# Scanning the decays once on compact rows and multiplying them into B and C before their transposes

## The chip, the cores and the metric

The kernel runs on one core of a Trainium2 chip. The metric is the device time of one launch in microseconds (us), and lower is better. Executions of one kernel spread by about 1% or more, and the medians of the same kernel differ by up to 1% (the kernel before: 140.49 to 141.62 us). So every experiment below was timed in rounds beside the kernel before on the same chip, and its ratio to that kernel is given with the median. A run that is more than 1.5% above the fastest of its kernel is counted as slow and is left out of the ratios; only fast runs are compared with fast runs.

Names: PE is TensorE, DVE is VectorE, ACT is ScalarE, POOL is GpSimd. SP and ACT also issue the loads. PSUM is where the matmuls of this kernel leave their results, HBM is the memory of the chip from which the loads come.

## The reference, cut to what matters

```python
# x (4, 8, 768, 32), a (4, 8, 768), B and C (4, 8, 768, 16), all fp32
la  = np.log(np.clip(a, 1e-6, 1.0))                  # decay of every token of every head
for c in chunks:                                     # state-space layer, chunk by chunk
    cum = np.cumsum(la[chunk]);  L = exp(cum_i - cum_j) * causal
    y   = ((C B^T) * L) x + (C state) * exp(cum)
    state = exp(sum la) * state + sum_j B_j x_j exp(cum_end - cum_j)
h   = y_as_3072_tokens_by_256 @ w_in                 # MLP: 256 -> 2048
out = gelu_tanh(h) @ w_out                           # 2048 -> 256
```

The kernel takes chunks of 128 tokens, so there are 4 batches of 6 chunks. In every chunk a decay factor is split in two: `r` (the product of decays from a token to the end of its chunk) scales B, and its inverse `pn` (up to a factor of the chunk) scales C. Both come out of a running product, a scan.

## The kernel before

The program builds a list of pieces of work with an engine, an estimated duration and a priority. A small scheduler (`run_order`) puts them into one order before anything runs; each engine then executes its own list in that order (in b_wo_first below PE stood 3.30 us at the entry that came next in its list; in b_fill_hole, with other work put ahead of that entry, PE was busy for 10.07 us of that window of 12.9 us instead of 7.79). Dummy matmuls ("fillers", 128x512, into a bank that nobody reads) are put into gaps of PE that the scheduler foresees in the first 22 us.

For every batch the parts that the change touches are these. The decays are loaded 16 times over, once for every state row, so that they lie in the layout [128 = head x state, 768 tokens]. DVE scans them in this layout, twice.

```python
def load_a(b, t0, t1):                       # 16-fold replicated: [0, N] is a stride of zero
    nc.sync.dma_start(out=d["a"][:, t0:t1],
        in_=bass.AP(tensor=a.tensor, offset=..., ap=[[S, H], [0, N], [1, t1 - t0]]))

def f_R(b, c0, c1):                          # DVE: clip, scan from the right, two small ones
    nc.vector.tensor_scalar(out=ac[:, s0:e1], in0=d["a"][:, s0:e1], ...)
    nc.vector.tensor_tensor_scan(out=d["r"][:, s0:s1][:, ::-1], data0=ac[...][:, ::-1], ...)
    ...
def f_P(b, c0, c1):                          # DVE: scan from the left
    nc.vector.tensor_tensor_scan(out=d["pn"][:, s0:s1], data0=a_cl[b % 2][:, s0:s1], ...)

def f_castbc(b, i, eng, r0, r1): ...         # B or C to bf16, token-major
def f_T(b, i): ...                           # PE: six 128x128 transposes into PSUM
def f_E(b, i, p0, p1):                       # DVE: out of PSUM, multiplied by r or pn
    nc.vector.tensor_tensor(out=tv(d[nm]), in0=d[("t", i)]..., in1=tv(d[("r", "pn")[i]]),
                            op=ALU.mult)
# then: F  (DVE)  C split by head parity -> ce        N (PE) B back to token-major
#       G  (PE)   Gram matmuls -> gb                  M (DVE) causal mask, PSUM -> m
#       Y  (PE)   output of a chunk -> yb             S, SP (DVE) running state
#       s1 (PE)   first MLP layer, line L391          s2 (PE) second MLP layer, line L409
```

Some short names are used below and in the expectations: "first MLP matmul" or s1 is the first `hp<-xm,w_in_sb` matmul, T the transposes of B and C, M0 the mask of chunk 0, and G, Y as above.

## Time and profile before

| | before |
|---|---|
| median (3 runs) | 141.21 us (141.12 to 141.3) |
| span of the profiled run | 140.0 us |
| busy PE / DVE / ACT / POOL | 121.4 / 78.3 / 80.5 / 17.0 us |
| read from HBM | 12.06 MB |
| first MLP matmul starts | 19.60 us |
| last matmul ends | 136.41 us |

The first view is the page's row of slices: 40 equal slices of the span (3.5 us each), each digit the busy share in tenths; PEclk is the granted clock of TensorE in tenths.

```profile
PE   6583799961599969899989999999999999999990
...
DVE  2538999709985499999799676788200000000011
...
PEclk9999999996558999999999999999999999999999
```

Counted from 0, PE is dense from slice 20 on. The losses lie before: the start, and a hole in slices 8 to 10; the clock falls in slices 9 to 12. DVE is nearly full from slice 14 to slice 21.

The second view is the chain of waits, the work that ended last followed back to its releasers, as shares of the span by engine.

```profile
PE 60%; DMA 17%; DVE 16%; ACT 2%; SPq 1%; issue 1%; DVEq 0%; ACTq 0%
```

Three of the longer pieces of the same chain in order of time (start, length, what):

```profile
2.74 8.09 DMA a_t<-in_a_dram
...
21.70 9.45 DMA a_t<-in_a_dram
...
41.38 6.25 DMA a_t<-in_a_dram
```

Three loads of the replicated decays make up the 17% of DMA. The third view is the timeline of DVE around the second of them (start, length, engine, line, what; in brackets the idle time before it and what ended it).

```profile
31.17 0.56 DVE L228 TENSOR_SCALAR ac_120<-a_t 128x768 f32<-128x768 f32 x1 [4.12 <-DMA a_t<-in_a_dram]
31.77 1.76 DVE L236 TENSOR_TENSOR_SCAN r_t<-ac_120,ends 128x768 f32<-128x768 f32 x1
...
33.72 0.55 DVE L214 CAST bc_551<-bc_t 128x768 bf16<-128x768 f32 x1
34.19 1.75 DVE L253 TENSOR_TENSOR_SCAN pn_t<-ac_120,headz 128x768 f32<-128x768 f32 x1
...
37.91 0.88 DVE L214 CAST w_out_sb<-wf 128x1024 bf16<-128x1024 f32 x1
```

The timeline of PE, with the first MLP matmul and the end of the wait in that stretch:

```profile
19.60 1.08 PE L391 MATMUL hp<-xm,w_in_sb 128*128 128x128 bf16 x16
...
34.33 0.82 PE L273 MATMUL hp<-ident,bc_551 128*128 128x128 bf16 x6 [3.83 <-DVE bc_551 L214]
```

The same stretch in the table of windows: start and end, length, then the busy time with the number of instructions for PE, PEld (weight loads), DVE, ACT and POOL, then the granted clock, the share of DMA and GB/s.

```profile
30.50:43.40 12.90, 7.28 (x64) 5.97 (x65) 10.54 (x17) 3.51 (x8) 4.21 (x6) 0.60 0.56 97
```

DVE stood 4.12 us for the decays of batch 1, then scanned. PE stood 3.83 us for the first cast of that batch, and in 12.9 us it was busy for 7.28 us at a mean clock of 0.60. The last w_out cast came only at 37.91.

### The profile page before, as it was taken

What the parts mean: (1) busy time and instruction counts of PE and PEld (TensorE: products, weight loads), DVE (VectorE), ACT (ScalarE), POOL (GpSimd) and SP (SyncE); (2) the same over time, 40 slices, a digit from 0 to 9 for tenths busy, and PEclk for the clock granted to TensorE, in tenths of its full rate; (3) what the DMA queues carried; (4) which work ended last, traced back from release to release, by engine and by line L of the source; (5) the groups of instructions that cost most, each with busy time, mean ns of one, the idle gap of its engine ahead of it and who ended that gap; (6) DMA issues with size and microseconds to landing.
All of it is one profiled execution on the core that took longest, in us unless ns stands there. A gap on an engine that the chain in (4) does not pass through costs nothing.

```text
span 140.0 us, 3321 instructions
## 1 busy us (share of the span) xinstructions
PE 121.4 (87%) x1380; PEld 94.4 (67%) x1380; DVE 78.3 (56%) x143; ACT 80.5 (58%) x161; POOL 17.0 (12%) x36
## 2 busy tenths in 40 slices
PE   6583799961599969899989999999999999999990
PEld 2141368751477857687867776777888888888870
DVE  2538999709985499999799676788200000000011
ACT  4124858670154844258835877687877777777210
POOL 7200023101810023112131110000000000000000
PEclk9999999996558999999999999999999999999999
DMA  2999999998705997898611010101011111111121
GB/s 64 243 211 326 308 275 265 223 162 146 110 21 148 218 158 141 178 254 155 96 37 42 0 37 5 37 0 42 0 37 42 37 37 37 42 37 37 62 90 37
DMA packets 40630, 15.41 MB, mean 110 GB/s; under 512 B 33832, under 2 KB 39080, under 8 KB 40616
## 3 DMA queue, kind: packets, MB, share of 16 engines
q1 hardware_dynamic: 39576, 14.82, 47.4%
q10 hardware_dynamic: 1040, 0.39, 1.1%
q8 instruction: 10, 0.16, 0.6%
q14 instruction: 4, 0.03, 0.1%
HBM read 12.06 MB, written 3.15 MB: 109 GB/s over the span
## 4 chain that ended last, share of the span: by engine, by line
PE 60%; DMA 17%; DVE 16%; ACT 2%; SPq 1%; issue 1%; DVEq 0%; ACTq 0%
PE o_ps L409 25%; PE hp L391 24%; DMA a_t<-in_a_dram 17%; DVE r_t L236 4%; DVE m L324 3%; PE yb L341 3%; PE gb L316 3%; PE hp L409 2%; DVE pn_t L253 2%; PE yb L335 1%; ACT gT L399 1%; PE hp L273 1%; DVE ch L285 1%; DVE bh L285 1%; DVE ac_118 L228 1%; DVE bc_551 L214 1%
## 5 line engine op out<-in xcount | busy, mean ns | idle before, releaser
L399 ACT ACTIVATE gT<-hp 128x512 bf16<-128x512 f32 x96 | 55.3, 598 | 25.2 <-PE hp L391 24.3
L391 PE MATMUL hp<-xm,w_in_sb 128*128 128x256 bf16 (+1 forms) x480 | 56.4, 255 | 0.4 <-ACT gT L399 0.2
L409 PE MATMUL o_ps<-w_out_sb,gT 128*128 128x256 bf16 x352 | 50.6, 277 | 1.1 <-ACT o_sb L416 1.1
L391 PEld LDWEIGHTS <-w_in_sb 128*128 128x128 bf16 x480 | 39.1, 99 | 6.7 <-issue 1.1
L409 PEld LDWEIGHTS <-gT 128*128 128x128 bf16 x384 | 36.6, 99 | 6.8 <-issue 1.7
L324 DVE TENSOR_TENSOR m<-gb,tri 128x1024 bf16<-128x1024 f32 x24 | 29.2, 1218 | 2.4 <-PE gb L316 2.4
L418 DVE COPY o_sb<-o_ps 128x256 f32<-128x256 f32 x2 | 0.8, 424 | 36.8 <-PE o_ps L409 36.8
L359 ACT ACTIVATE xm<-yb 128x256 bf16<-128x256 f32 x24 | 9.2, 382 | 6.3 <-PE yb L352 4.6
L590 PE MATMUL o_ps<-wz 128*128 128x512 bf16 x36 | 11.0, 436 | 1.3 <-DVE warm L124 1.3
L416 ACT ACTIVATE o_sb<-o_ps 128x256 f32<-128x256 f32 x20 | 7.6, 380 | 5.7 <-PE o_ps L409 5.4
L372 DVE SCALAR_TENSOR_TENSOR sp_new<-s_new,pend,bmask 128x256 bf16<-128x256 f32 x20 | 9.5, 477 | 0.2
L316 PE MATMUL gb<-ce,bh 32*128 32x256 bf16 x96 | 6.9, 278 | 2.1 <-DVE m L324 1.2
L210 ACT ACTIVATE w_in_sb<-wf 128x1024 bf16<-128x1024 f32 x4 | 4.2, 1057 | 4.8 <-DMA wf<-in_moe_w_in_dram 4.8
L316 PEld LDWEIGHTS <-bh 32*128 32x128 bf16 x96 | 2.7, 91 | 6.0 <-issue 5.2
L590 PEld LDWEIGHTS <-wz 128*128 128x128 bf16 x36 | 3.4, 107 | 4.9 <-issue 1.6
L273 PE MATMUL hp<-ident,bc_551 128*128 128x128 bf16 x12 | 1.6, 307 | 5.5 <-DVE bc_551 L214 3.8
L366 DVE SCALAR_TENSOR_TENSOR s_new<-s_new,pend,yb 128x64 f32<-128x64 f32 x16 | 4.4, 274 | 3.4 <-ACT xm L359 2.9
L309 ACT ACTIVATE bn<-yb 128x384 bf16<-128x384 bf16 (+2 forms) x9 | 4.1, 454 | 3.4 <-DVE w_out_sb L214 2.2
L335 PE MATMUL yb<-ch,sp_new 128*128 128x128 bf16 x40 | 5.7, 225 | 0.0
L273 PEld LDWEIGHTS <-bc_551 128*128 128x128 bf16 x12 | 1.2, 135 | 5.8 <-DVE bc_551 L214 4.9
L285 DVE TENSOR_TENSOR ch<-hp,pn_t 128x768 bf16<-128x768 bf16 (+3 forms) x6 | 4.1, 682 | 0.8 <-PE hp L273 0.8
L285 DVE TENSOR_TENSOR bh<-hp,r_t 128x768 bf16<-128x768 bf16 (+3 forms) x6 | 4.1, 680 | 0.6 <-PE hp L273 0.6
(147 smaller groups left out, 89.5 us busy)
## 6 DMA issues: line engine op xcount, KB each, us to landing
x_t<-in_x_dram SPq DMA_DIRECT2D x24, 128.0 KB, 4.3
out_dram<-o_sb SPq DMA_DIRECT2D x24, 128.0 KB, 1.7
wf<-in_moe_w_in_dram SPq DMA_DIRECT2D x4, 512.0 KB, 8.4
wf<-in_moe_w_out_dram SPq DMA_DIRECT2D x4, 512.0 KB, 8.0
bc_t<-in_C_dram SPq DMA_DIRECT2D x4, 384.0 KB, 6.4
a_t<-in_a_dram SPq DMA_DIRECT2D x3, 384.0 KB
bc_t<-in_B_dram SPq DMA_DIRECT2D x3, 384.0 KB, 6.8
bc_t<-in_B_dram ACTq DMA_DIRECT2D x1, 384.0 KB
```

Source lines behind the costliest of these rows:

```text
L236: nc.vector.tensor_tensor_scan(out=d["r"][:, s0:s1][:, ::-1], data0=ac[:, s0 + 1:s1 + 1][:, ::-1], data1=ef[:, ::-1], initial=1.0, op0=ALU ...
L285: nc.vector.tensor_tensor(out=tv(d[nm]), in0=d[("t", i)].rearrange("q (r p) -> q p r", r=R6)[:, p0:p1], in1=tv(d[("r", "pn")[i]]), op=ALU. ...
L316: nc.tensor.matmul(out=gb[:, g, 0:256], lhsT=d["bh"][32 * g:32 * g + 32, c * Q:(c + 1) * Q], rhs=d["ce"][32 * g:32 * g + 32, c].rearrange( ...
L324: nc.vector.tensor_tensor(out=m, in0=gram, in1=tri_b, op=ALU.mult)
L335: nc.tensor.matmul(out=y_ps[:, w], lhsT=sp[:, w * 128:(w + 1) * 128], rhs=d["ch"][:, c * Q:(c + 1) * Q], start=(w == 0), stop=False, skip_ ...
L359: nc.scalar.activation(xm[:, :, gc * Q:(gc + 1) * Q], y_ps, AF.Copy)
L372: nc.vector.scalar_tensor_tensor(out=sp_new.rearrange("p (g d) -> p g d", g=4), in0=state[("s", gc)].rearrange("p (o d) -> p o d", o=1).to ...
L391: nc.tensor.matmul(out=hp[:, j * nt:(j + 1) * nt], lhsT=w_in_sb[:, kc, fi * 128:(fi + 1) * 128], rhs=xm[:, kc, c0 * Q:c0 * Q + nt], start= ...
L399: nc.scalar.activation(gts[g][:, i * per:(i + 1) * per, 0:nt], hps.pop((g, i)).rearrange("p (j t) -> p j t", j=per), AF.Gelu_apprx_tanh)
L409: nc.tensor.matmul(out=ops[gc], lhsT=gts[g][:, fi, tt * Q:(tt + 1) * Q], rhs=w_out_sb[:, fi, :], start=(fi == 0), stop=(fi == NF - 1), ski ...
L416: nc.scalar.activation(o_sb, ops.pop(gc), AF.Copy)
L590: nc.tensor.matmul(out=zb, lhsT=wz[:, 0:128], rhs=wz, start=True, stop=True)
```

## The change

Intent: load the decays once, compactly (64 rows of 384, 0.1 MB instead of 1.57 MB), clip and scan them once for all batches, and only from the right. Small fp32 matmuls against an identity ("RT") bring the scan's result to token-major, one number for each token and head; `1/r` is a reciprocal. These factors are multiplied into B and C in the place of the casts, ahead of the transposes, so that what comes out of PSUM is only copied. Four more fp32 matmuls ("pp") spread the chunks' end factors `pend`. The order of loads changes, weight casts move to POOL, and the scheduler gets a rule for letting DVE and POOL stand still for a more urgent piece that is nearly ready. Much is cut here:

```diff
+    a_t = const.tile([64, HS], FP32, name="a_t")
+    nc.scalar.dma_start(out=a_t[0:32], in_=a_half[0])
+    load_bc(0, 1, nc.sync)
+    nc.scalar.dma_start(out=a_t[32:64], in_=a_half[1])
+    load_bc(0, 0, nc.sync)
 ...
-    def f_P(b, c0, c1):  ... (second scan, gone)
-    def f_castbc(b, i, eng, r0, r1):  ... (cast, gone)
+    def f_R():
+        nc.vector.tensor_tensor_scan(out=r_t[:, ::-1], data0=ac[:, 1:HS + 1][:, ::-1], ...)
+    def f_RT():                               # 12 fp32 matmuls
+        for r in range(R6):
+            for i in range(2):
+                nc.tensor.matmul(out=U[0]["rp"][64 * i:64 * i + 64, r],
+                                 lhsT=r6[32 * i:32 * i + 32, r], rhs=idf[...], ...)
+    def f_pp():                               # 4 fp32 matmuls
+        for b in range(batch):
+            nc.tensor.matmul(out=U[0]["pp"][:, b * CPB:(b + 1) * CPB], lhsT=selp[...], ...)
+    def f_mul(b, i, eng, r0, r1):             # in place of the cast
+        (nc.vector if eng == "DVE" else nc.gpsimd).tensor_tensor(
+            out=d["bc16"][:, i, r0:r1], in0=d["bc"]..., in1=w..., op=ALU.mult)
 ...
     def f_E(b, i, p0, p1, eng):
-        nc.vector.tensor_tensor(out=tv(d[nm]), in0=..., in1=tv(d[("r", "pn")[i]]), op=ALU.mult)
+        copy(eng, d[nm]..., d[("t", i)]...)
 ...
+    weng = [("POOL", "ACT", "POOL", "DVE"), ("POOL", "POOL", "POOL", "DVE")]   # w_in, w_out
 ...
+            if b == 0:      # first batch: both multiplies split between DVE and POOL
+                ms = [add("DVE", 0.6, f_mul, b, i, "DVE", 0, 4, deps=dp, prio=-62 - i),
+                      add("POOL", 0.7, f_mul, b, i, "POOL", 4, R6, deps=dp, prio=-62 - i)]
 ...
-    for t, fn in run_order(nodes, pools, idle=idle):
+    for t, fn in run_order(nodes, pools, idle=idle, wait=("DVE", "POOL")):
```

## The prediction

> **What bounds it now.** Time is a PE (TensorE) stream that starts late and is interrupted once. In the timeline the first matmul of the two-layer MLP starts at 19.6 us and the last ends near 136.4; span 140.0, median 141.2. From 80 us on the table of windows shows PE 100% busy. Two losses lie earlier.
> 1. Start: until 19.6 us PE does fillers and small matmuls. The chain there is DMA `a_t` (arriving 10.85), then DVE clip, scans, E, F, M in pieces, M for chunk 0 only at 12.19, M for chunk 1 at 17.86.
> 2. The hole 30.5-43.4 us. DVE waits 4.1 us (view of waits) for batch 1's `a_t`, issued at 21.7, landed 31.17, a 16-fold replicated 384 KB load; then in order clip 0.56, scan 1.76, cast, scan 1.75, cast 0.69, E 0.94, and only then the last `w_out` cast at 37.91, for which every second-layer group waits. PE does about 4.5 us of full-clock work in 12.9 us. [...] A hole of 2 us at 49-51.6 is the same scan again.
>
> **What changes.** Removed from DVE: about 7.4 us each of the r and p scans, 2.2 clips, 4.8 of B/C casts, three of four w_out casts (2.2). From DMA: 1.57 MB of replicated `a` becomes 0.1 MB. Added: one clip and 64x384 scan (0.35 + 0.96, as the 128x384 ones), 12 fp32 matmuls (estimate 1 us), reciprocals 0.5 + 1.3, multiplies in place of casts (estimate 0.9 each against 0.65, from E's 0.94). PSUM copies replace E at about equal cost. Net DVE 78 to about 62 us. POOL gains five weight casts, estimate 1.6 us each undisturbed (four times 0.40), ACT loses three.
>
> **New start (estimate).** a lands 3.3, scan ends 4.8, matmuls 5.9, C lands near 5.7, multiply 7.0, transposes, F, G0 near 9, M0 ends 10.6, Y0 11, first MLP matmul near 12, 7.5 us sooner. Then arrivals pace it: at the 2.36 us per x-plus-wo pair seen now, the last w_in lands near 14.5, the last w_out near 22-23, B/C of batch 1 near 27, all before PE runs dry.
>
> **Sum.** PE work left after 43.4 us is 93 us less about 3 us of waits, plus 18 us done before: 108 us. If after has done 12-14 us of it by 22-23 us and then runs dense with 1-2 us of gaps, PE ends near 118-119; tail 3.6, span to median 1.2: about 123.5 us, 12.5% less. About 8 us comes from closing the holes, the rest from the early start; the DVE saving itself is mostly off the critical path.
>
> **What the profile would show.** First MLP matmul at 11-14 us; no a_t wait on DVE after 4 us; PE clock 0.9+ throughout 20-60; a chain almost all PE after about 23 us; scan time about 1 us; DVE busy 60-65.
>
> **What would make it wrong.** POOL is slow: an x cast (0.40 alone) took 1.2-1.7 beside DVE casts and scans. [...] If weight casts take 3-4 us, x3 and w_out come late, and a new hole opens at 18-27 us (+3 to 6 us). In-order DVE waits (for the fourth w_in cast, before M2) could delay chunks 2 and 3.
>
> Range 119.5-129; faster 0.97, same 0.02, slower 0.01.

93 us less 3 us plus 18 us make 108 us of work on PE, which was to end near 118 to 119, and 3.6 and 1.2 us more make about 123.5 us. What the trace of the kernel before shows of the clock in the hole is 0.57, 0.50 and 0.65 from 32 to 36, 36 to 40 and 40 to 44 us. The trace of the kernel after has 1.57 us for the 12 fp32 matmuls (predicted 1), 0.46 and 1.04 us for the reciprocals (0.5 and 1.3), 0.95 to 1.08 us for a multiply of a whole batch on DVE (0.9), and 0.95 us for a copy of 128x768 out of PSUM on DVE, the time of E before.

## The result, and the profile after

| | before | after |
|---|---|---|
| median of this comparison (4 runs each) | 141.17 us | 129.51 us |
| all runs | 140.65 to 141.3 | 128.77, 129.07, 129.96, and a slow one of 130.76 |
| ratio of the fast runs | | 0.9163, 95% interval 0.9102 to 0.9225 |
| span of the profiled run | 140.0 us | 127.1 us |
| busy PE / DVE / ACT / POOL | 121.4 / 78.3 / 80.5 / 17.0 | 118.9 / 66.9 / 77.2 / 21.4 |
| read from HBM | 12.06 MB | 10.58 MB |
| first MLP matmul starts | 19.60 | 17.96 |
| last matmul ends | 136.41 | 123.82 |
| from one to the other | 116.8 | 105.9 |

A ratio here and below is the mean time of one kernel's fast runs over the mean of the other's fast runs of the same rounds, so it is not quite the ratio of the medians quoted beside it.

The change is 8.4% faster. The predicted direction was right. The predicted 123.5 us was not: the measured 129.5 us is just outside the range of 119.5 to 129.

First the slices of the page, 3.2 us each:

```profile
PE   6579899899999999999999999999999999999990
...
DVE  2354899877978799899956658665000000000001
...
PEclk9985559999999999999999999999999999999999
```

The chain of waits by engine:

```profile
PE 86%; DMA 3%; DVE 3%; ACT 3%; issue 1%; ACTq 0%; DVEq 0%
```

The window that answers to the hole shown before:

```profile
30.50:43.40 12.90, 12.90 (x198) 10.76 (x195) 10.99 (x16) 8.19 (x18) 2.96 (x7) 1.00 0.91 174
```

The hole is gone: PE is busy 12.90 of 12.90 us at full clock, and the chain is nearly all PE. That is the last row of the table: the stretch from the first MLP matmul to the last matmul fell from 116.8 to 105.9 us. What did not come is the early start. The clock's row shows where one cause lies: slices 3 to 5, from about 10 to 19 us, stand at half. The timeline of DVE in the first 20 us:

```profile
5.59 0.35 DVE L245 TENSOR_SCALAR ac<-a_t 64x384 f32<-64x384 f32 x1 [2.05 <-DMA a_t<-in_a_dram]
5.97 0.95 DVE L249 TENSOR_TENSOR_SCAN r_t<-ac,ends 64x384 f32<-64x384 f32 x1
...
9.17 0.69 DVE L294 TENSOR_TENSOR bc_181<-bc_t,pt 128x512 bf16<-128x512 f32 x1
9.78 1.11 DVE L294 TENSOR_TENSOR bc_181<-bc_t,rt 128x512 bf16<-128x512 f32 x1
...
18.18 1.45 DVE L235 CAST w_in_sb<-wf 128x1024 bf16<-128x1024 f32 x1
```

And the timeline of PE:

```profile
7.07 1.57 PE L260 MATMUL hp<-idf,r_t 32*64 32x32 f32 x24 [2.21 <-DVE r_t L249]
8.57 1.89 PE L650 MATMUL o_ps<-wz 128*128 128x512 bf16 x4
10.39 1.87 PE L281 MATMUL hp<-pe_112,selp 64*128 64x6 f32 x8
12.19 1.46 PE L309 MATMUL hp<-ident,bc_181 128*128 128x128 bf16 x12
...
16.92 1.03 PE L650 MATMUL o_ps<-wz 128*128 128x512 bf16 x2
...
17.96 1.36 PE L428 MATMUL hp<-xm,w_in_sb 128*128 128x128 bf16 x16
```

Four things are to be seen. The clip, and with it everything, waited until 5.59 for the compact decays. The four fillers took 1.89 us, which is half pace: the kernel before ran four of them in 1.04 us at 13.68. The pp matmuls stand in front of the transposes for 1.87 us. And the last two fillers, 1.03 us at half pace, stand directly in front of the first MLP matmul (two transposes between).

That it is half, although 1.89 is less than twice 1.04, is an estimate from longer runs of fillers in the same traces. The kernel after took 3.59 us for its first eight, so four more cost 1.70 us; the kernel before took 1.90 us for eight at 16.84, so four more cost 0.86 us. By that, one more filler takes about 0.43 us at half pace and 0.22 us at full pace. In the expectations below, cold stands for half pace.

The trace records two rows for each of the fp32 matmuls (24 for the 12 of RT, 8 for the 4 of pp). Their price was 1.57 us for RT and 1.87 us for pp, against an estimate of 1 us for RT in the prediction and none for pp. The 1.87 us is the price at half pace: in the run best below, where PE was at full pace from 6.39 us on, pp took 1.02 us, while RT, which ran before that, took 1.54 us.

Some instructions of DVE took longer beside POOL. Two lines of the timeline of POOL:

```profile
9.22 1.12 POOL L294 TENSOR_TENSOR bc_181<-bc_t,pt 128x256 bf16<-128x256 f32 x1 [4.88 <-DVE pt L267]
...
18.04 1.04 POOL L233 CAST w_out_sb<-wf 128x1024 bf16<-128x1024 f32 x1 [0.37 <-DMA wf<-in_moe_w_out_dram]
```

The w_in cast took 1.45 us at 18.18, after POOL had begun to cast w_out at 18.04; the same cast took 0.68 us in a_first below, where no POOL cast overlapped it, and 0.68 us in control, where it began 0.36 us before POOL's. The C multiply on DVE began 0.05 us before POOL's part of it and took 0.69 us; the B multiply of the same shape began while POOL's part of C still ran, took 1.11 us, and ended 0.55 us after that part (10.34). The B multiply reads two tiles (`bc_t` and `rt`), the cast only one; why either took longer here, no run shows.

### The profile page after: what moved, and what is told of

Read it like the earlier page. It is cut to its first block, busy times and chain, and to the rows that moved or that the text cites. A ratio compares the mean times of both kernels' runs of the same rounds, so it can differ in the third digit from the quotient of the medians.

```text
span 127.1 us, 3322 instructions
## 1 busy us (share of the span) xinstructions
PE 118.9 (94%) x1393; PEld 95.2 (75%) x1394; DVE 66.9 (53%) x109; ACT 77.2 (61%) x159; POOL 21.4 (17%) x45
## 3 DMA queue, kind: packets, MB, share of 16 engines
HBM read 10.58 MB, written 3.15 MB: 108 GB/s over the span
## 4 chain that ended last, share of the span: by engine, by line
PE 86%; DMA 3%; DVE 3%; ACT 3%; issue 1%; ACTq 0%; DVEq 0%
PE hp L428 33%; PE o_ps L446 31%; PE gb L352 4%; PE yb L377 4%; PE o_ps L650 3%; DMA a_t<-in_a_dram 3%; PE hp L446 3%; PE hp L309 3%; ACT gT L436 2%; PE yb L371 2%; PE hp L281 1%; PE hp L260 1%; PE yb L338 1%; DVE m L360 1%; DVE sp_new L409 1%; DVE r_t L249 1%
## 5 line engine op out<-in xcount | busy, mean ns | idle before, releaser
L428 PE MATMUL hp<-xm,w_in_sb 128*128 128x256 bf16 (+1 forms) x480 | 54.6, 253 | 0.3 <-ACT gT L436 0.2
L446 PE MATMUL o_ps<-w_out_sb,gT 128*128 128x256 bf16 x352 | 48.6, 273 | 0.1
L409 DVE SCALAR_TENSOR_TENSOR sp_new<-s_new,pend,bmask 128x256 bf16<-128x256 f32 x20 | 10.3, 514 | 0.6
L650 PE MATMUL o_ps<-wz 128*128 128x512 bf16 x17 | 8.2, 626 | 1.3 <-DVE warm L153 1.3
L650 PEld LDWEIGHTS <-wz 128*128 128x128 bf16 x18 | 2.0, 129 | 4.0 <-issue 2.7
L446 PE MATMUL hp<-w_out_sb,gT 128*128 128x256 bf16 x32 | 3.8, 272 | 0.2 <-ACT gT L436 0.2
L371 PEld LDWEIGHTS <-sp_new 128*128 128x128 bf16 x40 | 3.6, 98 | 0.5
L235 DVE COPY ch<-hp 128x768 bf16<-128x768 bf16 x4 | 3.8, 948 | 0.0
L260 PEld LDWEIGHTS hp<-idf,r_t 32*64 32x64 f32 x24 | 1.5, 201 | 3.1 <-issue 3.1
## 6 DMA issues: line engine op xcount, KB each, us to landing
x_t<-in_x_dram SPq DMA_DIRECT2D x24, 128.0 KB, 3.8
out_dram<-o_sb SPq DMA_DIRECT2D x24, 128.0 KB, 1.7
```

The source lines that it names most:

```text
L371: nc.tensor.matmul(out=y_ps[:, w], lhsT=sp[:, w * 128:(w + 1) * 128], rhs=d["ch"][:, c * Q:(c + 1) * Q], start=(w == 0), stop=False, skip_ ...
L409: nc.vector.scalar_tensor_tensor(out=sp_new.rearrange("p (g d) -> p g d", g=4), in0=state[("s", gc)].rearrange("p (o d) -> p o d", o=1).to ...
L428: nc.tensor.matmul(out=hp[:, j * nt:(j + 1) * nt], lhsT=w_in_sb[:, kc, fi * 128:(fi + 1) * 128], rhs=xm[:, kc, c0 * Q:c0 * Q + nt], start= ...
L446: nc.tensor.matmul(out=ops[gc], lhsT=gts[g][:, fi, tt * Q:(tt + 1) * Q], rhs=w_out_sb[:, fi, :], start=(fi == 0), stop=(fi == NF - 1), ski ...
L650: nc.tensor.matmul(out=zb, lhsT=wz[:, 0:128], rhs=wz, start=True, stop=True)
```

## The experiments

There are two questions. Why did the start not come 7.5 us sooner, and what closed the hole? My theory for the first: the decays arrive late because they are issued behind other loads, and PE work that the critical path does not need (pp, fillers) stands in the in-order queue at half clock. My rivals: the split of the multiplies with POOL, and the arrival of weights. For the second: my theory at prediction was the late w_out cast; the rivals were the decay loads, the scans, and the scheduler's new rule.

Eighteen runs were made, two of them of the kernel after without a change. The table gives the medians and ratios; the texts are below. Clauses of three recorded expectations (warm5, all, a_mul_wi) are cut for the reason given beside the prediction; what is left of the theory of all and a_mul_wi is that DVE took longer beside POOL (`ce` of chunk 1: 1.26 us in a_first beside a POOL cast, 0.47 us in after). "First" is the start of the first MLP matmul in the profiled run, "rest" the time from there to the end of the last matmul. The profiled run is one of the timed ones and can lie at either end of their spread.

| label | based on | median | ratio to before | first | rest |
|---|---|---|---|---|---|
| control | after | 128.79 | 0.9159 | 17.54 | 106.1 |
| control2 | after | 129.72 | 0.9177 | 18.29 | 107.1 |
| a_first | after | 126.19 | 0.8966 | 15.85 | 105.3 |
| pp_late | after | 128.77 | 0.9146 | 17.28 | 106.7 |
| warm5 | after | 128.00 | | 17.01 | 105.6 |
| a_pp2 | after | 127.75 | 0.9053 | 16.48 | 107.1 |
| a_pp2_nf | after | 127.44 | 0.9110 | 15.61 | 107.0 |
| all | after | 128.24 | 0.9160 | 15.42 | 106.7 |
| a_zb_nf | after | 126.08 | 0.8978 | 14.32 | 106.7 |
| a_nf | after | 126.29 | 0.8975 | 14.17 | 106.7 |
| a_mul_wi | after | 126.01 | 0.8987 | 13.77 | 106.5 |
| best | after | 125.68 | 0.8896 | 13.01 | 106.9 |
| b_pref | before | 138.38 | 0.9712 | 19.74 | 113.0 |
| b_wo_first | before | 140.73 | 1.0070 | 20.06 | 116.2 |
| b_fill_hole | before | 141.65 | 1.0096 | 20.08 | 116.8 |
| b_wait | before | 147.16 | 1.0436 | 20.78 | 120.0 |
| scan_back | after | 144.94 | 1.0240 | 18.18 | 122.3 |
| scan_back2 | after | 132.48 | 0.9373 | 19.06 | 109.5 |

### The start

**control.** The kernel after, with a comment added.

```diff
+# unchanged
```

> The changed kernel again, untouched, so that the other runs of this call have it on the same chip. Both theories: 128.5 to 131 us, first MLP matmul near 18 us in its trace, the granted clock at half in roughly 8 to 18.5 us in the profiled run, perhaps not in every run.

Measured: 128.79 us (128.08 to 129.66), ratio 0.9159. So the result stands. The profiled run also taught a caution. Here is a line of its timeline of PE:

```profile
8.67 1.89 PE L650 MATMUL o_ps<-wz 128*128 128x512 bf16 x4
```

And its window from 8.2 to 18.6 us:

```profile
8.20:18.60 10.40, 10.39 (x81) 6.01 (x79) 7.52 (x13) 3.92 (x10) 6.12 (x8) 1.00 1.11 304
```

The granted clock stands at 1.00, and yet the four fillers took the 1.89 us of half pace, as in the profiled run of after with its recorded 0.51 in the same window. So in this case the pace of known matmuls tells the state; the record alone does not.

**a_first.** Both halves of the decays are issued first, one on each of two queues.

```diff
-    nc.scalar.dma_start(out=a_t[0:32], in_=a_half[0])
-    load_bc(0, 1, nc.sync)
-    nc.scalar.dma_start(out=a_t[32:64], in_=a_half[1])
+    nc.sync.dma_start(out=a_t[0:32], in_=a_half[0])
+    nc.scalar.dma_start(out=a_t[32:64], in_=a_half[1])
+    load_bc(0, 1, nc.sync)
```

> Both halves of the decay load go out first, one on each queue, ahead of the first C load; nothing else moves. Theory (the start chain sets the end): decays land near 3.3 us in place of 5.5, the scan ends near 4.7, PE is not idle for 2.2 us before the fp32 matmuls, the clock is not halved in 8 to 18 us, the first MLP matmul comes 2 to 3.5 us earlier (14.5 to 16) and the time falls by about as much: 126 to 128. Rival (weight loads and casts pace the first 25 us): the start moves, the time stays at 129 +- 0.7.

Measured: 126.19 us (125.45 to 126.72), ratio 0.8966; against control, 2.6 us less. The time and the start are as the theory had them; its clock is not, as is seen below. The clip in its timeline of DVE:

```profile
3.46 0.34 DVE L245 TENSOR_SCALAR ac<-a_t 64x384 f32<-64x384 f32 x1
```

The fillers and the first MLP matmul in its timeline of PE:

```profile
6.43 1.89 PE L650 MATMUL o_ps<-wz 128*128 128x512 bf16 x4
...
15.85 1.06 PE L428 MATMUL hp<-xm,w_in_sb 128*128 128x128 bf16 x16
```

The clip started at 3.46 instead of 5.69 in control, without a wait. The loads landed 2.0 and 2.3 us after their issue, against 2.8 and 4.2 us in after, where the second half was issued at 1.28 with C already on its way. The first MLP matmul came 1.69 us sooner than in control; the rest of the gain came later (105.3 us from there to the last matmul instead of 106.1). PE had no idle stretch before the fp32 matmuls any more (they began at 4.93), and still the fillers took 1.89 us and the transposes 1.46 us. So the idle 2.2 us is not what halves the pace, at least not alone.

**pp_late.** The pp matmuls are moved behind the first Gram, into an unused half of a Gram bank.

```diff
-        U[0]["pp"] = rp[:, 256:256 + NCH]
+        U[0]["pp"] = gb[:, 0, 256:256 + NCH]
+    for n, after in [(ppn, Gn[0]), (pendn, Mn[0])]:
+        fns.remove(n.fn)
+        fns.insert(fns.index(after.fn) + 1, n.fn)
```

> The four fp32 matmuls that spread the chunk-end decays (1.87 us in the trace) move from in front of the first transposes to behind the first Gram matmuls, with their copy on DVE behind the first masked multiply; the order of all else is unchanged. Theory: transposes start near 10.4 in place of 12.2 us, first MLP matmul 1 to 1.8 us earlier, time 127.7 to 128.7. Rival (weights pace the start): transposes move, time unchanged at 129 +- 0.7.

Measured: 128.77 us (127.95 to 129.08), ratio 0.9146; the same as control. A miss, and partly a spoiled test: the transposes did start at 10.71 instead of 12.29, but M0 then stood 1.07 us until 14.14. The record puts that wait down to a POOL cast that ended at 14.14; the pp matmuls, which write into the same tile that M0 reads, had ended at 14.03. So it gave the time back on the next step. It shows only that this way of moving pp gains nothing.

**warm5.** Five more fillers at the very start, so that PE has work until the fp32 matmuls begin.

```diff
+        if t0 == 0.0:
+            n += 5
```

> Five more filler matmuls at the start, so that PE has work until about 6 to 7 us, when the fp32 matmuls begin; decays still land near 5.5. Theory that the halved clock of 8 to 18.5 us comes from the idle stretch of 2.2 us and costs time: the clock stays full, the stretch from the fp32 matmuls to the first MLP matmul shrinks by 1.5 to 2.5 us, time 127 to 128. Rival ([...]it costs nothing as the chain waits on other engines): clock still halved, or full with the time at 129 +- 0.7.

Measured: a median of 128.0 us, but three of the four runs count as slow beside a single one of 125.57 us, and the profiled run is one of the slow ones. In that run the four fillers at 8.73 took 1.04 us, full pace, and the transposes at 11.29 took 1.46 us, half pace: the pace fell between them although PE was recorded busy. The profiled run of pp_late, a fast one, shows such a fall too: two fillers took 0.60 us at 13.97 and 1.03 us at 16.24, and PE waited between them for no more than 0.39 us.

**a_pp2, a_pp2_nf, all.** Built on a_first with the pp matmuls late in another bank; without the fillers after the first eight; and with the first batch's multiplies all on DVE and POOL's w_in casts on ACT.

```diff
+        U[0]["pp"] = gb[:, 3, 256:256 + NCH]      # a_pp2: and ordered as in pp_late
-        if t0 > 22.0 or n < 1:
+        if t0 > 1.0 or n < 1:                     # a_pp2_nf, all: no later fillers
-                      add("POOL", 0.7, f_mul, b, i, "POOL", 4, R6, deps=dp, prio=-62 - i)]
+                      add("POOL", 0.7, lambda: None, deps=dp, prio=-62 - i)]     # all: DVE does 0..R6
```

> Decays first (as a_first, 126.2 us) and the four spreading matmuls behind the first Gram matmuls, this time in PSUM columns behind all that the masked multiply reads, so that it can not be held up by them as it was in pp_late (1.07 us of wait there). Theory (the length of the start chain sets the end, one to one): transposes at about 8.4 in place of 10.05 us, first MLP matmul 14 to 15, time 124.5 to 125.5. Rival (weight loads and casts now pace the start: the second w_in cast on ACT and POOL begins only at 13.8 us): first MLP matmul earlier by under 0.7, time 125.5 to 126.5.

> As a_pp2, without any filler matmul after the first eight. Theory that fillers sized for the full clock but run at half of it stand in the way (four took 1.89 us in front of the spreading matmuls, two took 1.03 in front of the first MLP matmul): another 0.5 to 1 us earlier start, time 124 to 125. Rival (fillers keep PE from going cold and so are worth their time): PE stays at half clock for longer, time equal to or above a_pp2.

> As a_pp2_nf, and batch 0's multiplies all on DVE (6 rows each, near 0.95 us; split with POOL they took 0.69 and 1.11 beside POOL's 1.12 and 1.06), and the two w_in casts of POOL on ACT. Theory that POOL's work [...]slows DVE (chunk 1's ce took 1.26 us beside a POOL cast, against 0.47): DVE's ce, sp and cast in 10-20 us at their short times, another 0.5 to 1.5 us, time 123 to 124.5. Rival ([...]ACT becomes the limit): time within 0.5 us of a_pp2_nf.

Measured: a_pp2 127.75 us (two of four runs slow), ratio 0.9053; a_pp2_nf 127.44 us (127.12 to 127.68), ratio 0.911; all 128.24 us (127.27 to 128.71), ratio 0.916. The theory misses in all three, and none shows a gain over a_first; of the rivals, only that of a_pp2_nf held (PE stays at half pace for longer, and the ratio is no better than that of a_pp2). In a_pp2 the transposes started at 7.74, but M0 only at 12.54, after the pp matmuls ended at 12.43: a wait of 2.41 us which the trace puts down to them. In all three the first 16 MLP matmuls ran at half pace (1.91 us), and PE came to full pace only at about 18.5 us with fillers (a_pp2) and at about 20 us (a_pp2_nf) and 18 us (all) without.

**a_zb_nf, a_nf.** The wait for pp is avoided by putting pp into the fillers' own bank (a_zb_nf); a_nf is a_first with only the later fillers left out.

```diff
+    U[0]["pp"] = zb[:, 0:NCH]                     # a_zb_nf
-        if t0 > 22.0 or n < 1:
+        if t0 > 1.0 or n < 1:                     # both
```

> Decays first, no filler after the first eight, and the spreading matmuls behind the first Gram matmuls and writing to the fillers' own PSUM bank. In pp_late, a_pp2 and a_pp2_nf the first masked multiply stood until those matmuls were through (12.56 us against 10.7 when Gram was done), which hid what the move was worth. Theory (chain length sets the end): masked multiply 0 near 10.7, first MLP matmul 13.5 to 14.5, time 125 to 126 in spite of a cold PE. Rival (weights pace the start, and the clock): MLP matmuls start near 14 but wait for w_in casts to 15-16, PE cold until 18 or later, time 126.5 to 127.7 as a_pp2_nf.

> As a_first, without any filler after the first eight: fillers are the only difference. If the half clock costs time and the fillers are what ends it (a_first's PE was at full pace from about 14 us, the run without fillers a_pp2_nf only from about 20): transposes earlier by up to 0.9 us, but the first 32 MLP matmuls at 1.9 us per 16 in place of 1.06, time 126.8 to 127.8. If fillers only stand in the way: first MLP matmul earlier, time 125 to 126.

Measured: a_zb_nf 126.08 us (125.67 to 126.54), ratio 0.8978; a_nf 126.29 us with one slow run, ratio 0.8975. The first MLP matmul came at 14.32 and 14.17, 1.5 to 1.7 us sooner than in a_first, and the time stayed that of a_first. The first 16 MLP matmuls took 1.91 us again, against 1.06 us in a_first. So neither pp nor the fillers in front are a loss that can simply be taken away: most of what was saved went to the slow pace. a_nf lies between the two ranges that were expected, a_zb_nf just above the range of its theory.

**a_mul_wi, best.** Built on a_first: the first batch's multiplies all on DVE; POOL's w_in casts on ACT, both in a_mul_wi and only the third in best.

```diff
-                ms = [add("DVE", 0.6, f_mul, b, i, "DVE", 0, 4, deps=dp, prio=-62 - i),
-                      add("POOL", 0.7, f_mul, b, i, "POOL", 4, R6, deps=dp, prio=-62 - i)]
+                ms = [add("DVE", 0.6, f_mul, b, i, "DVE", 0, R6, deps=dp, prio=-62 - i),
+                      add("POOL", 0.7, lambda: None, deps=dp, prio=-62 - i)]
-        wi_n[q] = add(e, wdur[e], f_wi, q, e, ...)
+        wi_n[q] = add(e, wdur[e], f_wi, q, ("ACT" if e == "POOL" else e), ...)   # a_mul_wi
+        wi_n[q] = add(e, wdur[e], f_wi, q, ("ACT" if q == 2 else e), ...)        # best
```

> As a_first (126.2 us), with batch 0's multiplies all on DVE and POOL's two w_in casts on ACT; fillers stay. Theory ([...]ce of chunk 1 took 1.26 us beside a POOL cast, 0.47 elsewhere): that ce near 0.5, Gram 1 near 14.3 in place of 15.07, time 125.2 to 125.9. Rival (no gain, ACT gets the delay instead): 126 to 127.

> a_first with batch 0's multiplies all on DVE and only the third w_in cast moved from POOL to ACT, so that no cast stands in front of bh on ACT (1.3 us of PE wait in a_mul_wi). If the end still follows the start: first MLP matmul near 13 us, time 124.5 to 125.3. If w_out's arrival (22.1 to 23.8 us in a_mul_wi) now paces it: first MLP matmul near 13 us, time 125.3 to 126.3, no better than a_mul_wi or a_first.

Measured: a_mul_wi 126.01 us (125.27 to 126.64), ratio 0.8987; best 125.68 us (124.86 to 126.52, six runs), ratio 0.8896. The unchanged kernel after (control2) had 129.72 us and 0.9177, so best takes about 3% less than after, and it is the fastest version found. a_mul_wi fell into the range of its rival, best into the second of its two ranges. Four lines of best's timeline of PE:

```profile
6.39 1.04 PE L650 MATMUL o_ps<-wz 128*128 128x512 bf16 x4
...
8.41 1.04 PE L309 MATMUL hp<-ident,bc 128*128 128x128 bf16 x12
...
13.01 1.06 PE L428 MATMUL hp<-xm,w_in_sb 128*128 128x128 bf16 x16
...
20.61 0.60 PE L446 MATMUL o_ps<-w_out_sb,gT 128*128 128x256 bf16 x4 [0.60 <-POOL w_out_sb L233]
```

And one of its timeline of POOL:

```profile
21.79 1.04 POOL L233 CAST w_out_sb<-wf 128x1024 bf16<-128x1024 f32 x1 [0.88 <-DMA wf<-in_moe_w_out_dram]
```

The start is now 13.01, close to the predicted 12. The profiled run is the fastest of the six, with 124.86 us; the median is 125.68 us. At 20.61 PE waits for a cast of w_out, and the casts wait for their loads; the fourth one starts on DVE at 23.40, again after a wait for its load. Of the 2.84 us that best starts sooner than a_first, 1.29 us arrived at the end of the last matmul in the profiled runs (119.90 against 121.19). In the medians it is 0.5 us, and by the ratios about 1 us, with intervals that overlap. Of the 1.55 us that were lost on the way, PE's two waits for casts of w_out (0.60 and 0.36 us) are the larger part. So the arrival of the weights takes back much of a start that is earlier than that of a_first (15.85); how much, these runs do not settle.

In both of these profiled runs PE was at full pace from about 6.4 us on, with the same order of PE as a_first, which was at half pace there. That is worth more than the edit. Fillers, pp and transposes took 1.04, 1.02 and 1.04 us in best against 1.89, 1.87 and 1.46 us in a_first, 2.1 us less, and PE in a_first was never idle from 4.93 until the transposes were done, so no multiply held it up there. Gram of chunk 0 started 2.1 us sooner (9.99 against 12.10); only the last 0.7 us of the 2.84 came after it, where a_first waited 0.71 us for `ce` beside POOL's w_in cast. No experiment shows that the edit brought the full pace.

**control2.** The kernel after once more.

```diff
+# unchanged, again
```

> The changed kernel untouched, on the same chip as best: 128 to 130.5 us.

Measured: 129.72 us (128.78 to 130.38), ratio 0.9177 (0.9121 to 0.9232). It agrees with the result.

### The hole

**b_wo_first.** The kernel before, with the last w_out cast moved ahead of batch 1's clip.

```diff
+    fns.remove(wo_n[3].fn)
+    fns.insert(fns.index(Rn[(1, 0)].fn), wo_n[3].fn)
```

> The kernel before, with one DVE instruction moved: the last w_out cast goes in front of the clip that waits for batch 1's decays. Theory (the hole at 30.5-43.4 us is second-layer work held back by that cast standing behind a wait in DVE's in-order queue): second-layer matmuls begin near 29 us, PE stays busy to about 37, its clock is not halved, time 133 to 136.5. Rival (the hole is the late B/C and decays of batch 1 themselves, and only a cheaper decay path closes it): time 138.5 to 141.5.

Measured: 140.73 us (140.29 to 141.61), ratio 1.0070 (0.9981 to 1.0159). No gain, and this refutes the prediction's reading of the hole. Its timeline of DVE:

```profile
28.25 0.69 DVE L214 CAST w_out_sb<-wf 128x1024 bf16<-128x1024 f32 x1 [0.76 <-DMA wf<-in_moe_w_out_dram]
31.11 0.56 DVE L228 TENSOR_SCALAR ac<-a_t 128x768 f32<-128x768 f32 x1 [2.16 <-DMA a_t<-in_a_dram]
```

And of PE:

```profile
34.26 0.82 PE L273 MATMUL hp<-ident,bc 128*128 128x128 bf16 x6 [3.30 <-DVE bc L214]
```

The cast is done by 29, and PE stands 3.30 us just the same, because the next entry in its queue is batch 1's transposes. They wait for a cast on DVE that comes behind the scan, which comes behind the load.

**b_fill_hole.** Further: the second-layer matmuls of chunks 0 to 2 are also moved ahead of batch 1's transposes in PE's order.

```diff
+    early = [wo_n[3].fn]                          # and s2 of chunks 0..2, with their evictions
+    k = fns.index(Rn[(1, 0)].fn);  fns.insert(k, early[0])
+    k = fns.index(Tn[(1, 0)].fn);  fns[k:k] = early[1:]
```

> The kernel before, with the order changed in one place: the last w_out cast in front of the wait for batch 1's decays, and the second layer of chunks 0 to 2 (with its evictions) in front of batch 1's first transposes in PE's queue. In b_wo_first PE stood at those transposes until 34.3 us, so moving the cast alone gave nothing. Theory now (the hole is PE's in-order queue standing at batch 1's transposes, which wait for decays that landed at 31.1 us, and it could be filled by order alone): about 4.5 us of second-layer work in 30-35 us, clock not halved or less long, time 134.5 to 137. Rival (the work moved only leaves a hole later): 139.5 to 141.5.

Measured: 141.65 us (141.4 to 142.41), ratio 1.0096 (1.0015 to 1.0176). The rival held (its range ended at 141.5): the hole was filled, and the time did not fall. The window, against 7.28 us at a clock of 0.60 before:

```profile
30.50:43.40 12.90, 10.07 (x138) 8.15 (x136) 11.57 (x17) 6.32 (x14) 4.04 (x6) 1.00 0.72 127
```

The hole had moved to the next batch. The timeline of PE:

```profile
50.43 0.40 PE L316 MATMUL gb<-ce,bh 32*128 32x256 bf16 x4 [4.00 <-DVE m L324]
```

And of DVE:

```profile
46.48 0.56 DVE L228 TENSOR_SCALAR ac<-a_t 128x768 f32<-128x768 f32 x1 [3.58 <-DMA a_t<-in_a_dram]
```

PE now waits 4.00 us for a mask on DVE which stands behind the clip of batch 2, which waited 3.58 us for its decays. My reading is that the MLP work that PE can do in a wait is limited by what the chunks have delivered, so that filling one wait brings the next one forward. The chain of DVE, with the load at its head, was the limit, and PE's holes its symptom.

**b_pref.** The kernel before with its scans, but the decay loads of batches 1 to 3 issued sooner, each into a tile of its own.

```diff
-            d["a"] = ld.tile([128, S], FP32, name="a_t")
+            d["a"] = const.tile([128, S], FP32, name=f"a_t{b}")
+    for n, after in [(an[1], win_l[3]), (an[2], xl[9]), (an[3], bcn_l[(2, 1)])]:
+        fns.remove(n.fn)
+        fns.insert(fns.index(after.fn) + 1, n.fn)
```

> The kernel before, with the decays of each batch in a tile of their own and their loads moved forward in the queue (batch 1 behind the w_in loads, batch 2 behind the tenth x load, batch 3 behind batch 2's C load): the scans remain, the waits for decays (4.1 + 2.0 + about 2 us) go. If those waits made the holes: time 134 to 137.5, transposes of batch 1 near 31 us in place of 34.3. If the scans and the arrival of B and C are enough to make them: transposes of batch 1 still at 33 or later, time 139 to 141.5.

Measured: 138.38 us (136.3 to 139.03, two of them slow), ratio of the fast runs 0.9712 (0.963 to 0.9795). It lies between the two ranges that were expected. The clip of batch 1 in its timeline of DVE starts without a wait, and PE, which waits only 0.21 us before the first transposes of that batch, still stands before the second:

```profile
29.38 0.55 DVE L228 TENSOR_SCALAR ac<-a_t 128x768 f32<-128x768 f32 x1
```

```profile
35.92 0.69 PE L273 MATMUL hp<-ident,bc 128*128 128x128 bf16 x6 [2.08 <-DVE bh L285]
```

So the net gain of earlier decay loads is about 4 us by the ratio of the fast runs (3 to 5 us by its interval); moving these loads also moved others, which is in this number. The rest of the hole stays.

**scan_back.** The kernel after, with the DVE work of clip and scans put back for batches 1 to 3 (on constants, so nothing waits for a load), and the scheduler not told of it.

```diff
+        if b and i == 1:
+            nc.vector.tensor_scalar(out=dmy[:, 0], in0=one, scalar1=1e-6, scalar2=1.0, ...)
+            for k in range(2):
+                nc.vector.tensor_tensor_scan(out=dmy[:, 1 + k], data0=dmy[:, 0], data1=one, ...)
```

> The changed kernel, with a clip and two scans of 768 elements (0.56 + 1.76 + 1.75 us, on constants, results unused) put in front of the multiplies of each of batches 1 to 3: 12.2 us of DVE work more, no load and no wait. If DVE's scans in the serial chain made the holes of the kernel before: PE waits of 2 to 4 us again near each batch's start, time 133 to 138. If the scans were off the critical path, as the prediction put it, and the holes came from waiting for the replicated loads: time 129 to 131.

Measured: 144.94 us (144.15 to 145.41), ratio 1.0240, above both ranges. After had 129.72 us, so 12.2 us of DVE work cost 15 us. The waits before the transposes of two batches, from its timeline of PE:

```profile
34.92 0.82 PE L318 MATMUL hp<-ident,bc 128*128 128x128 bf16 x6 [3.17 <-DVE bc L303]
...
53.32 0.82 PE L318 MATMUL hp<-ident,bc 128*128 128x128 bf16 x6 [3.93 <-DVE bc L303]
```

The work alone, without a load to wait for, brings the holes back. But 15 us is more than the whole change gains, so this could not be the right price. The scheduler had ordered PE's queue for a DVE that is done sooner.

**scan_back2.** The same, with the scheduler told of the 4.07 us for each batch.

```diff
-                ms = [add("DVE", 0.85, f_mul, b, i, "DVE", 0, R6,
+                ms = [add("DVE", 0.85 + (4.07 if i == 1 else 0.0), f_mul, b, i, "DVE", 0, R6,
```

> As scan_back (144.9 us), but the scheduler counts 4.07 us more for the first multiply of batches 1 to 3, so PE's queue is ordered for it. If the DVE work itself is what the change saved in the middle: 134 to 140 us. If scan_back's loss was mostly the wrong order and the work can be hidden: 129.5 to 133.

Measured: 132.48 us (132.13 to 133.65), ratio 0.9373 (0.9308 to 0.9438), in the second of the two ranges. After had 0.9177, so the scans cost some 3 us when the order of work allows for them, and 15 us when it does not. What was left of a hole, in its table of windows:

```profile
43.40:56.00 12.60, 10.49 (x126) 7.77 (x124) 11.20 (x15) 6.58 (x14) 2.07 (x4) 0.86 1.01 192
```

**b_wait.** The kernel before with nothing but the scheduler's new rule.

```diff
-def run_order(nodes, pools, hop=0.2, same=0.06, idle=None):
+def run_order(nodes, pools, hop=0.2, same=0.06, idle=None, wait=()):
+        if eng in wait:
+            soon = [(e, m) for e, m in cand[eng] if t < e < t + n.dur - 0.1 and m.prio < n.prio - 5]
+            ...
-    for t, fn in run_order(nodes, pools, idle=idle):
+    for t, fn in run_order(nodes, pools, idle=idle, wait=("DVE", "POOL")):
```

> The kernel before, scans and all, with only one thing of the change: the scheduler is told that VectorE and GpSimd also stand still while they wait, so that it orders their work by when its inputs are there. My theory (the hole of batch 1 closes because the scans and the waits for the decays leave VectorE's serial chain) expects little of this order alone: 139.5 to 141.8 us, ratio 0.99 to 1.005, and PE still standing 2 us or more at batch 1's transposes between 30 and 36 us. The rival (part of the closed hole is due to the new rule of order, not to the removed work) expects 137.5 to 139.3 us and a hole of batch 1 under 2 us.

Measured: 147.16 us (146.28 to 147.73), ratio 1.0436 (1.0365 to 1.0506). Both expectations miss: I had allowed for no effect or a gain, and it is a loss of 6 us. The hole is there as before, in its timeline of PE:

```profile
33.78 0.82 PE L284 MATMUL hp<-ident,bc 128*128 128x128 bf16 x6 [2.98 <-DVE bc L225]
```

So the rule alone is not what closes the hole. Whether it helps the kernel after, where DVE has less to do, no run shows.

## Why the prediction was wrong, point by point

**The direction and the middle were right.** The prediction put the end of PE at 118 to 119 us with a start of 12 us, so 106 to 107 us between. The measured stretch is 105.9 us, and 116.8 us before. The hole is closed, the chain is 86% PE, and PE's clock from 20 us on is full (1.00 from 20 to 60 us and from 60 to 123), as announced. DVE is busy 66.9 us instead of the announced 60 to 65. That the middle came out so close is in part luck: the change takes away the loads, the scans and the late casts at once, so its time could not tell which of them made the hole, and one of the reasons that the prediction gave, the late cast, fails below.

**The step that failed is "New start (estimate)": "first MLP matmul near 12, 7.5 us sooner".** The mechanism, an earlier start by compact decays, was there; the size was wrong. The start came at 17.96, 1.6 us sooner than before. Term by term, in the profiled run:

| term | predicted | measured | lag gained here | in best |
|---|---|---|---|---|
| scan of the decays ends | 4.8 | 6.92 | 2.1 | 4.76 |
| RT matmuls end | 5.9 | 8.64 | 0.6 | 6.45 |
| C multiplied (POOL's part ends last; in best all on DVE) | 7.0 | 10.34 | 0.6 | 7.95 |
| Gram of chunk 0 starts | 9 | 14.24 | 1.9 | 9.99 |
| M0 ends | 10.6 | 15.99 | 0.2 | 11.63 |
| first MLP matmul | 12 | 17.96 | 0.6 | 13.01 |

The first lag was the landing of the decays, 3.3 predicted and 5.5 measured, as the second half was issued behind the first, at 1.28, when the load of C was already under way. This was shown by a_first, which issued both halves ahead of C and B: the scan ended 2.2 us sooner than in control, the first MLP matmul came 1.69 us sooner, and the time fell by 2.6 us. The second large lag is that the prediction let the transposes follow the multiplies at once. The pp matmuls (1.87 us), fillers at half pace and transposes at half pace (1.46 us for 12; 1.04 us in best, where PE was at full pace) stood between; the prediction had not put pp on PE's path at all. That these take this time is read from the trace. That removing them alone would give it back is not so: pp_late was no faster than control, and a_zb_nf and a_nf no faster than a_first, as the first MLP matmuls then ran at half pace or M0 waited. The last column shows what was left where the decays came first and PE was at full pace: the predicted chain, 1.0 us late, with fillers and pp still in it. So the terms that failed are the landing of the decays, as a_first shows, and the pace of PE, which the prediction did not foresee for the start; the second is read from traces, as no experiment switched the pace alone.

**The arrivals were nearly right in time and wrong in price.** The prediction had the last w_out near 22 to 23 us, and in best its fourth cast started at 23.40, after a wait for the load. But it assumed that this would come "before PE runs dry". In best, with a start at 13.01, PE waited 0.60 and 0.36 us for casts of w_out at 20.6 and 24.2 us, was busy for 11.57 of the 12.54 us from 17.96 to 30.5 (12.03 us in after), and the time of this run was 124.86 us. So a start that came near to the predicted one was not seen to give 123.5 us.

**"And only then the last `w_out` cast at 37.91, for which every second-layer group waits" is refuted as the cause of the hole** by b_wo_first: the cast came at 28.25 and the time was the same.

**"The DVE saving itself is mostly off the critical path" holds only in part.** scan_back and scan_back2 put back only DVE work, 12.2 us of it, and lost 15 and about 3 us. With an order made for it, then, most of that work was hidden, as the prediction had it, but not the last 3 us; with an order made without it, it cost more than it took. DVE's serial chain was on the path through its order, and b_fill_hole shows that work for PE in one wait does not shorten it.

**A small term:** the prediction added 1.2 us from span to time, by comparing the span of one run with the median of others. In the profiled runs themselves it is 2.0 us before (142.03 against 140.0) and 1.7 us after.

**POOL's casts**, the announced risk, were not slow: 1.03 to 1.31 us each, against the estimate of 1.6 us. The price came on DVE, where the w_in cast beside one of them took about twice its time (1.45 against 0.68 us).

What stays open: of the 11 us that the middle lost, earlier decay loads gave about 4 us in the kernel before (b_pref), and the scans cost about 3 us in the kernel after (scan_back2). These two were measured in different kernels and need not add up. The rest, some 4 us, was not taken apart; the moved w_out casts, the smaller traffic of loads, and the rule of order together with less DVE work are candidates. What keeps PE at half pace from 8 to 18 us is open too. In the profiled run of after it was recorded busy for 10.03 of the 10.40 us from 8.2 to 18.6 us, at a recorded clock of 0.51, with small fp32 matmuls among its work (pp, 1.87 us) and just before (RT, 1.57 us). That the idle stretch before them is the cause was for warm5 to tell, and it could not. The idle 2.2 us are not enough of an answer (a_first), and neither are the fp32 matmuls alone: a_mul_wi and best had the same ones in the same order and ran at full pace from 6.4 us on.

## What to carry to other kernels

When a stage is made shorter, look at what else stands in the in-order queues in front of the next step: here one half of a small load, issued 0.5 us later behind another, held the start up by about 2 us. And before a piece of work in front is called a loss, take it away: four small fp32 matmuls stood there for 1.87 us, and moving them gained nothing. A hole on PE is to be read back to the engine whose chain is late, as filling it with other work here only moved it to the next batch. Before the price of some removed work is named, put it back with the scheduler knowing of it: the same work cost 15 us or 3 us.
